# Attention head start regrouped: four tiles in one group, masks by matmul there, and a new order of the whole queue

## The chip, the cores and the metric

The kernel runs on one core of a Trainium2 chip. The metric is device time in microseconds (us), median of several runs.

## What is computed

Two stages follow each other. The first is attention with a local window of 96 keys and 8 global keys, causal, with a distance bias per head; the second is an FFN whose hidden layer is the maximum of three projections.

```python
B, H, S, D = 4, 8, 768, 64
scores = scale * q @ k.T                       # per batch and head
is_global = pos[None, :] < 8
is_local = (rel >= 0) & (rel < 96)             # rel = query - key
keep = is_global | is_local
dist = where(is_global & ~is_local, 96, abs(rel))
scores = scores - slopes[h] * dist             # slopes 2**-(h+1)
scores = where(keep, scores, -1e9)
a = softmax(scores)
x = (a @ v).reshape(3072, 512)                 # tokens x (heads x 64)
h = max(x @ w1, x @ w2, x @ w3)                # 512 -> 768
out = h @ w_out                                # 768 -> 512
```

## The kernel before

The 3072 tokens are 24 tiles of 128, six to a batch. Because of the window, a tile of queries needs only its own keys and those of the tile before (tile t = 0 of a batch: its own alone); the 8 global keys are copied over the first 8 keys of the previous tile, which the window never reaches.

One queue, the string SCHEDULE (L25), sets the order of everything. Each word is a unit: a letter and numbers, the last of which often picks the engine (0 ACT, 1 DVE, 2 POOL). Every engine takes its instructions in this order; SP issues nearly all DMAs in it. The units:

- l: load a part of q or k for a group of neighbouring tiles (`load_part`, L151). Tokens are dealt to partitions so that each partition reads `sz` neighbouring tokens in one run of `sz` x 256 bytes. c casts it to bf16 (`cast_part`, L178), x transposes it on TensorE and evicts it into qkT (`u_x`, L226). Groups (L91) are [first tile, tiles]: [0,2], [2,2], [4,2], [6,4], [10,2].
- L, C, X: the same for single tiles 12 to 23 (L160, L185, L245); X with 4 is a DMA transpose issued by SP. v and C with middle number 1: load and cast v.
- K: wmask, the factor exp(-slope x distance) for a head, on ACT (L297). B: the same bias as an addend for the scores (`u_B`, L291). G, V: copy global keys and values.
- S: scores of a tile for four heads (one g of two) into a PSUM tile sp, then one exp on ACT to P (`u_S`, L268). With its last number 1 the bias is first put into sp by a matmul (L275), and M then does nothing; otherwise M multiplies P by wmask on DVE (`u_M`, L302). In the old queue six of the score units of tiles 0 to 3 have the 1.
- A: P times v and a column of ones, then division on DVE to xb (`u_A`, L311). T: transposes xb to xT (`u_XT`, L335), on TensorE or, with 4, by DMA.
- w, W: load and cast w1 to w3. w g.j loads projection j: g = 0 the first 256 hidden columns, g = 1 the other 512, which two W units cast. o, Q: w_out.
- F c.f.j: projection j of the 128 hidden columns f for the tiles of chunk c: 4 matmuls into one of three PSUM buffers h; j = 0 is evicted by ACT, j = 1 and 2 by a maximum on DVE (`u_F1`, L355). O: second layer of one tile and its store (`u_F2`, L385). E: the last four tiles (L390).
- D: n matmuls on zeros (L432).

Chunks (L89) are 4, 2, 2, 4, 4, 4, 4 tiles: F units work on 512 or 256 columns.

[...] two tiles of two banks for scores and attention output (tags sp0, sp1), three buffers of one bank (tag h, used by F, O and early transposes) and one (tag tp).

Of the kernel before, what the change touches and what calls it, by code (L numbers as in the profile page):

```python
# [12 lines left out]
FP32 = mybir.dt.float32  # L13
# [12 lines left out]
    K0 K1 K2 K3 K4 K5 l1.0 l1.1 D0.3 c0.0.2 B0.1 B1.1 B2.1 B3.0 K6 B4.1 B5.1 c0.1.1 c1.0.2 x0.0.4 B6.1  # L26
    B7.1 x0.1.4 S0.0.1 v0 l2.0 l2.1 K7 S0.1.1 G0.0 S1.0.1 S1.1.0 x1.0.3 c1.1.2 M0.0 M0.1 M1.0 v1 x1.1.4
    C0.1.2 v2 A0.1 G1.2 S2.0.1 M1.1 c2.0.2 x2.0.1 C1.1.1 S2.1.0 G2.2 S3.0.1 M2.0 M2.1 C2.1.1 T0.1 S3.1.1
    M3.0 M3.1 c2.1.2 v3 A1.0 C3.1.0 w0.0 V1.2 x2.1.2 w1.0 A2.1 V2.2 A3.0 T1.0 T2.1 T3.1 W1.0.1 W0.0.0
    G3.2 S4.0.0 S4.1.0 F0.0.0 F0.1.0 M4.0 F0.2.0 F0.3.0 G4.1 S5.0.0 M4.1 S5.1.0 w0.1 W0.1.1 w0.2 W0.2.2  # L30
    V3.2 F0.0.1 F0.1.1 F0.0.2 F0.1.2 v4 C4.1.0 A4.0 V4.2 w1.1 W1.1.2 W2.0.0 F0.4.0 F0.5.0 M5.0 M5.1 w1.2
    W1.2.2 v5 W2.1.0 T4.0 F0.2.1 F0.3.1 l3.0 l3.2 F0.4.1 l3.1 c3.0.2 c3.2.2 F0.5.1 o2 C5.1.0 A5.1 l3.3
    F0.2.2 Q2.2 F0.3.2 W2.2.0 o0 T5.0 F0.4.2 o1 F0.5.2 x3.0.0 F1.0.0 F1.1.0 c3.1.1 F1.2.0 x3.2.0 Q0.2
    F1.0.1 F1.1.1 F1.2.1 l4.0 l4.1 c3.3.0 F1.0.2 F1.1.2 F1.2.2 x3.1.2 x3.3.1 F1.3.0 F1.4.0 Q1.2 F1.3.1
    S6.0.0 S6.1.0 v6 v7 v8 G6.0 F1.3.2 F1.5.0 v9 c4.0.1 F1.4.1 S7.0.0 S7.1.0 G7.2 v10 M6.0 M6.1 M7.0
    M7.1 O0.0.0 F1.4.2 c4.1.1 C6.1.2 C7.1.2 L12 F1.5.1 S8.0.0 S8.1.0 x4.0.0 O0.1.0 A6.0 x4.1.2 A7.1 V7.2
    F1.5.2 v11 T6.0 O0.2.0 T7.1 G8.2 C8.1.2 S9.0.0 S9.1.0 G9.1 v12 v13 O0.3.0 F2.0.0 F2.1.0 S10.0.0 M8.0
    M8.1 M9.0 M9.1 S10.1.0 C9.1.2 L13 L14 F2.0.1 F2.1.1 F2.0.2 A8.0 C12.0.1 F2.1.2 G10.2 O1.0.0 V8.2
    A9.1 X12.1 M10.0 M10.1 C10.1.0 C11.1.0 F2.2.0 S11.0.0 S11.1.0 M11.0 M11.1 L15 F2.3.0 F2.4.0 O1.1.0
    V9.2 A10.1 F2.2.1 V10.2 T8.0 F2.3.1 F2.5.0 T9.0 A11.1 F2.4.1 T10.0 F2.2.2 F2.3.2 T11.1 F2.4.2  # L40
    S12.0.0 S12.1.0 F2.5.1 C13.0.2 C14.0.2 C15.0.1 X13.4 F3.0.0 F3.1.0 F3.0.1 G12.1 C12.1.0 F3.2.0
    F3.1.1 F3.2.1 S13.0.0 S13.1.0 F2.5.2 v14 C13.1.0 C14.1.2 M12.0 M12.1 F3.0.2 F3.1.2 X14.4 F3.2.2
    X15.4 G13.2 M13.0 M13.1 S14.0.0 S14.1.0 F3.3.0 F3.4.0 F3.5.0 M14.0 M14.1 G14.1 A12.0 A13.1 F3.3.1
    F3.4.1 F3.5.1 S15.0.0 M15.0 S15.1.0 G15.0 v15 V13.2 L16 L17 v16 T12.4 v17 M15.1 O2.0.0 C15.1.0 A14.0
    V14.2 F3.3.2 F3.4.2 T13.4 F3.5.2 C16.1.0 C16.0.2 X16.3 T14.4 C17.0.2 A15.1 X17.4 O2.1.0 S16.0.0
    S16.1.0 G16.1 L18 V15.2 L19 T15.1 M16.0 O3.0.0 M16.1 F4.0.0 F4.1.0 F4.0.1 F4.1.1 C18.0.2 L20 C19.0.2
    A16.1 F4.2.0 F4.3.0 S17.0.0 S17.1.0 F4.2.1 F4.0.2 F4.3.1 v18 M17.0 v19 M17.1 X18.3 X19.4 C20.0.0
    V16.2 F4.1.2 C17.1.2 O3.1.1 A17.1 F4.2.2 F4.3.2 S18.0.0 M18.0 S18.1.0 M18.1 F4.4.0 T16.4 T17.4
    F4.4.1 C18.1.2 C19.1.1 F4.4.2 X20.4 G18.1 S19.0.0 S19.1.0 F4.5.0 L21 M19.0 M19.1 v20 F4.5.1 A18.0
    T18.4 F4.5.2 A19.1 T19.4 V19.1 C21.0.1 X21.4 G19.1 L22 C22.0.2 L23 X22.4 O3.2.1 O3.3.0 O4.0.1  # L50
    S20.0.0 S20.1.0 M20.0 G20.0 O4.1.0 F5.0.0 F5.1.0 F5.2.0 S21.0.0 S21.1.0 G21.2 F5.0.1 F5.1.1 M20.1
    M21.0 F5.3.0 F5.0.2 F5.1.2 F5.2.1 F5.2.2 v21 C20.1.1 C21.1.2 F5.4.0 S22.0.0 M21.1 S22.1.0 C23.0.0
    F5.3.1 M22.0 M22.1 F5.5.0 F5.3.2 A20.0 V20.2 G22.2 v22 F5.4.1 X23.4 v23 F5.5.1 T20.4 A21.1 V21.1
    T21.4 F5.4.2 F5.5.2 S23.0.0 S23.1.0 M23.0 O4.2.0 M23.1 C22.1.2 A22.0 C23.1.0 O4.3.0 V22.2 T22.4
    A23.1 T23.4 O5.0.1 O5.1.0 O5.2.1 O5.3.0 F6.0.0 F6.1.0 F6.0.1 F6.0.2 F6.2.0 F6.3.0 F6.4.0 F6.1.1
    F6.2.1 F6.1.2 F6.3.1 F6.4.1 F6.2.2 F6.3.2 F6.5.0 F6.4.2 F6.5.1 F6.5.2 E
# [4 lines left out]
def kernel(  # L61
# [27 lines left out]
    sizes = [4, 2, 2, 4, 4, 4, 4]  # L89

    GROUPS = [[0, 2], [2, 2], [4, 2], [6, 4], [10, 2]]  # L91
# [8 lines left out]
    NSTART = sizes[0]  # L100
# [21 lines left out]
    zeros = persist.tile([128, 512], BF16, name="zeros")  # L122
# [3 lines left out]
    bias = persist.tile([128, 2, 2, 2, 3, 128], BF16, name="bias")  # L126
    NVA = 4
    va_ring = [persist.tile([128, H * 65], BF16, name=f"va{i}") for i in range(NVA)]
    va_first = [persist.tile([128, H * 65], BF16, name=f"vaf{i}") for i in range(2)]
    kg8 = [persist.tile([128, NP, NG], BF16, name=f"kg8_{i}") for i in range(2)]  # L130
# [4 lines left out]
    xT = {}  # L135
    va, masked = {}, {}
# [7 lines left out]
    def part(n, s):  # L144

        T0, sz = GROUPS[n]
        jn = {2: 4, 4: 2, 6: 1}[sz]
        a, x = divmod(s, 4 // jn)
        return divmod(T0, NT) + (sz, a, x * jn, jn)

    def load_part(n, s):  # L151

        bb, t0, sz, a, j0, jn = part(n, s)
        r = raw_pool.tile([128, 2 * DM], FP32, name="rawp", tag="raw")
        r = r[:, 0:sz * jn * 128].rearrange("i (h x) -> i h x", h=2 * jn)
        raw["p", n, s] = r
        src = (q, k)[a][bb, 2 * j0:2 * (j0 + jn), t0 * 128:(t0 + sz) * 128, :]
        nc.sync.dma_start(out=r, in_=src.rearrange("h (i e) d -> i h (e d)", e=sz))
# [19 lines left out]
    def cast_part(n, s, how):  # L178
        bb, t0, sz, a, j0, jn = part(n, s)
        qk = cast_pool.tile([128, 2 * DM], BF16, name="qkp", tag="qkb")  # L180
        qk = qk[:, 0:sz * jn * 128].rearrange("i (e h d) -> i e h d", e=sz, d=D)
        qb["p", n, s] = qk
        copies[how](qk, raw["p", n, s].rearrange("i h (e d) -> i e h d", e=sz))  # L183
# [42 lines left out]
    def u_x(n, s, how):  # L226
# [14 lines left out]
        for (lo, hi, pool, tag, copy), tp in zip(halves, tps):  # L241

            copy(dst[:, lo:hi], tp.rearrange("c e j i -> c j i e"))  # L243
# [24 lines left out]
    def u_S(T, g, how):  # L268
# [3 lines left out]
        if how:  # L272

            for hh in range(2):
                nc.tensor.matmul(sp[:, hh, :, 0:n], identb,  # L275
                                 bias[:, g, hh, :, 0:2] if t else bias[:, g, hh, :, 2:3],
                                 start=True, stop=False, skip_group_check=True)
        for ds in range(2 if t else 1):
            for j2 in range(2):
                jp = 2 * g + j2  # L280
                for hh in range(2):
                    hsl = slice(64 * hh, 64 * hh + 64)
                    nc.tensor.matmul(sp[:, hh, j2, ds], qT(T - ds, 1)[hsl, jp], qT(T, 0)[hsl, jp],  # L283
                                     start=not how, stop=True, skip_group_check=True)
        P = p_pool.tile([128, 4, 2, 128], BF16, name="P", tag="P")
        Pt[T, g] = P
        masked[T, g] = how
# [3 lines left out]
    def u_B(h, how):  # L291
        g, hp = divmod(h, 4)
        j2, hh = divmod(hp, 2)
        mul = (nc.scalar.mul, nc.vector.tensor_scalar_mul, nc.gpsimd.tensor_scalar_mul)[how]
        mul(bias[:, g, hh, j2], rbase, -slopes[h] / scale)

    def u_K(h):  # L297
        g, hp = divmod(h, 4)
        j2, hh = divmod(hp, 2)
        nc.scalar.activation(wmask[:, g, 2 * hh + j2], rbase, AF.Exp, bias=0.0, scale=-slopes[h])  # L300

    def u_M(T, g):  # L302
        P = Pt[T, g]
        if masked[T, g]:
            return
        if T % NT:
            nc.vector.tensor_mul(P, P, wmask[:, g, :, 0:2])  # L307
        else:
            nc.vector.tensor_mul(P[:, :, 0], P[:, :, 0], wmask[:, g, :, 2])

    def u_A(T, how):  # L311

        b, t = divmod(T, NT)
        op = psS.tile([128, 2, 512], FP32, name="op", tag=f"sp{how}")
        for g in range(2):
            P = Pt[T, g]
            for j2 in range(2):
                for hh in range(2):
                    h = 4 * g + 2 * j2 + hh
                    i = 2 * hh + j2  # L320
                    o = op[:, g, (2 * j2 + hh) * 65:(2 * j2 + hh) * 65 + 65]
                    nc.tensor.matmul(o, P[:, i, 0], heads(va[T])[:, h], start=True, stop=(t == 0),  # L322
                                     skip_group_check=True)
                    if t:
                        nc.tensor.matmul(o, P[:, i, 1], heads(va[T - 1])[:, h], start=False, stop=True,  # L325
# [4 lines left out]
        o4 = op[:, :, 0:260].rearrange("p g (h e) -> p g h e", e=65)  # L330
        nc.vector.reciprocal(rz, o4[:, :, :, 64])
        nc.vector.tensor_tensor(out=x.rearrange("p (g h) d -> p g h d", g=2), in0=o4[:, :, :, 0:64],  # L332
                                in1=rz[:, :, :, None].to_broadcast([128, 2, 4, D]), op=ALU.mult)

    def u_XT(T, how):  # L335
        c, i = where[T]
        if i == 0:
            xT[c] = xT_pool.tile([128, NP, len(chunks[c]) * 128], BF16, name="xT", tag="xT")
        if how == 4:
            nc.sync.dma_start_transpose(out=xT[c][:, :, i * 128:(i + 1) * 128],  # L340
                                        in_=xb[T].rearrange("p h d -> p (h d)"))
# [8 lines left out]
        copies[how](xT[c][:, :, i * 128:(i + 1) * 128], tp)  # L350
# [4 lines left out]
    def u_F1(c, f, j):  # L355
        W = len(chunks[c]) * 128
        if f == 0 and j == 0:
            ht[c] = ht_pool.tile([128, NF, W], BF16, name="ht", tag="ht")
        ps = psH.tile([128, W], FP32, name="h", tag="h")
        for dm in range(4):  # L360
            nc.tensor.matmul(ps, w123[f // 2][:, dm, j, (f % 2) * 128:(f % 2) * 128 + 128],  # L361
                             xT[c][:, dm], start=(dm == 0), stop=(dm == 3))
        if j == 0:
            h01 = h01_pool.tile([128, W], BF16, name="h01", tag="h01")
            h01s[c, f] = h01
            nc.scalar.copy(h01, ps)  # L366
        elif j == 1:
            nc.vector.tensor_max(h01s[c, f], h01s[c, f], ps)  # L368
# [141 lines left out]
```

The softmax here doesn't subtract the row's maximum and nothing guards it: scores larger than these inputs give would overflow.

## Time and profile before

| what | us |
|---|---|
| median of 3 runs | 180.45 (180.34 to 180.5) |
| span of the profiled execution | 178.5 |
| outside the span (median less span) | 1.95 |
| first FFN matmul (h, L361) | 23.27 |
| L361: 491 matmuls recorded, chain share | 53% |
| L376: second layer, chain share | 16% |
| DVE: 36 mask products L307, mean | 0.716 |
| ACT: 40 exps of 128x1024 L288, mean | 1.027 |

The span runs from the first to the last instruction of the core. Busy time of TensorE includes the modelled end of each matmul; starts in the chain of waits are the better measure of what one matmul costs in a stream. Single long rows of the timeline, such as "x8", merge several instructions.

### The profile page before, as it was taken

The numbers are of one execution on the slowest core, as the hardware profiler recorded it, in microseconds if no ns is written. First come the engines' busy times: TensorE is split into PE (matmuls) and PEld (weight loads), VectorE is DVE, ScalarE is ACT, GpSimd is POOL, SyncE is SP. The second block draws the span as 40 slices with busy tenths as digits, with TensorE's granted clock in tenths as the row PEclk, the third lists the DMA queues.
The fourth block names the chain that finished last, engine by engine and source line by source line (L and its number), as shares of the span: only waits on it lengthen the run. The fifth ranks groups of instructions, "written<-read, shape, count | busy, mean of one in ns | idle before, by whom it ended". The sixth has DMA issues, their size and how long they took to land.

```text
span 178.5 us, 3963 instructions
## 1 busy us (share of the span) xinstructions
PE 167.1 (94%) x1529; PEld 95.9 (54%) x1551; DVE 119.1 (67%) x237; ACT 103.2 (58%) x160; POOL 37.4 (21%) x65
## 2 busy tenths in 40 slices
PE   3599799999999999999999999999999999999991
PEld 0455645458866677845555555454454555444451
DVE  4519975977796689748978448978358986137610
ACT  4867898646689958555753936351862543440131
POOL 4255203543343012210006024100020401000000
PEclk9999999999999999999999999999999999999998
DMA  5999999999998899899544999988989664700015
GB/s 139 292 270 243 357 321 383 319 361 356 252 194 229 218 254 227 142 204 234 92 90 122 167 253 231 145 172 152 182 156 300 123 129 147 252 12 4 0 47 190
DMA packets 83587, 35.52 MB, mean 199 GB/s; under 512 B 66160, under 2 KB 78320, under 8 KB 83568
## 3 DMA queue, kind: packets, MB, share of 16 engines
q1 hardware_dynamic: 83424, 35.20, 83.6%
q8 instruction: 12, 0.20, 0.5%
q10 hardware_dynamic: 144, 0.07, 0.1%
q14 instruction: 7, 0.06, 0.1%
HBM read 25.17 MB, written 6.29 MB: 176 GB/s over the span
## 4 chain that ended last, share of the span: by engine, by line
PE 88%; ACT 3%; DVE 2%; POOL 2%; issue 1%; DMA 1%; POOLq 0%; ACTq 0%
PE h L361 53%; PE po L376 16%; PE sp L283 7%; PE op L322 3%; PE op L325 3%; PE tpp L239 3%; PE xtp L349 2%; ACT wmask L300 2%; PE sp L275 2%; DMA out_dram<-ost 1%; DVE qkT L243 1%; DVE xb L332 1%; ACT ost L382 1%; ACT P L288 1%; PE tp L261 1%
## 5 line engine op out<-in xcount | busy, mean ns | idle before, releaser
L361 PE MATMUL h<-xT,w 128*128 128x512 bf16 (+1 forms) x491 | 99.2, 348 | 0.7 <-issue 0.2
L361 PEld LDWEIGHTS <-w 128*128 128x128 bf16 x504 | 47.0, 98 | 40.4 <-ACT w L427 0.2
L288 ACT ACTIVATE P<-sp 128x1024 bf16<-128x1024 f32 (+1 forms) x48 | 43.4, 954 | 20.4 <-PE sp L283 20.2
L368 DVE TENSOR_TENSOR h<-h,h 128x512 bf16<-128x512 bf16 (+1 forms) x42 | 25.2, 609 | 25.6 <-PE h L361 15.5
L366 ACT CAST h<-h 128x512 bf16<-128x512 f32 (+1 forms) x42 | 21.6, 532 | 21.5 <-PE h L361 21.3
L376 PE MATMUL po<-wo,ht 128*128 128x512 bf16 (+2 forms) x147 | 33.1, 362 | 0.5
L370 DVE TENSOR_TENSOR ht<-h,h 128x512 bf16<-128x512 bf16 (+1 forms) x42 | 25.0, 606 | 3.7 <-PE h L361 3.0
L307 DVE TENSOR_TENSOR P<-P,wmask 128x1024 bf16<-128x1024 bf16 x36 | 24.8, 716 | 3.6 <-ACT P L288 3.5
L382 ACT COPY ost<-po 128x512 f32<-128x512 f32 (+2 forms) x20 | 11.2, 564 | 18.4 <-PE po L376 11.2
L376 PEld LDWEIGHTS <-ht 128*128 128x128 bf16 x156 | 14.0, 98 | 13.8
L332 DVE TENSOR_TENSOR xb<-op,rz 128x512 bf16<-128x512 f32 x24 | 16.6, 691 | 0.8
L283 PEld LDWEIGHTS <-qkT 64*128 64x128 bf16 x352 | 10.2, 96 | 10.0 <-issue 8.0
L283 PE MATMUL sp<-qkT 64*128 64x128 bf16 x352 | 15.2, 223 | 0.4 <-DVE xb L332 0.4
L322 PEld LDWEIGHTS <-P 128*128 128x128 bf16 x192 | 12.5, 97 | 2.7 <-ACT P L288 0.2
L221 POOL COPY va<-vaf 8x260 int32<-8x260 int32 x14 | 6.3, 449 | 34.7 <-PE op L325 34.7
L198 POOL CAST qkb<-raw 128x1024 bf16<-128x1024 f32 x7 | 7.2, 1037 | 27.6 <-DMA raw<-in_k_dram 27.6
L322 PE MATMUL op<-va,P 128*128 128x65 bf16 x160 | 12.4, 193 | 0.3 <-ACT va L189 0.2
L239 PE MATMUL tpp<-identb,qkp 128*128 128x128 bf16 x96 | 8.5, 246 | 4.0 <-POOL qkp L183 3.5
L325 PEld LDWEIGHTS <-P 128*128 128x128 bf16 x160 | 10.4, 97 | 1.8 <-issue 0.2
L239 PEld LDWEIGHTS <-qkp 128*128 128x128 bf16 x96 | 7.0, 112 | 5.8 <-POOL qkp L183 4.4
L325 PE MATMUL op<-va,P 128*128 128x65 bf16 x128 | 9.9, 193 | 0.1
L243 ACT COPY qkT<-tpp 128x1024 bf16<-128x1024 bf16 (+1 forms) x9 | 7.9, 873 | 3.4 <-PE tpp L239 3.4
(66 smaller groups left out, 107.7 us busy)
## 6 DMA issues: line engine op xcount, KB each, us to landing
rawv<-in_v_dram SPq DMA_DIRECT2D x24, 256.0 KB, 4.9
out_dram<-ost SPq DMA_DIRECT2D x23, 256.0 KB, 2.3
rawp<-in_q_dram SPq DMA_DIRECT2D x6, 512.0 KB, 7.3
rawp<-in_k_dram SPq DMA_DIRECT2D x6, 512.0 KB, 7.7
wst<-in_moe_w_dram SPq DMA_DIRECT2D x3, 1024.0 KB, 10.3
raw<-in_q_dram SPq DMA_DIRECT2D x12, 256.0 KB, 4.2
raw<-in_k_dram SPq DMA_DIRECT2D x12, 256.0 KB, 4.7
wst<-in_moe_w_dram SPq DMA_DIRECT2D x3, 512.0 KB, 8.6
```

Source lines behind the costliest of these rows:

```text
L239: nc.tensor.transpose(tp[:, e, j - lo], qb["p", n, s][:, e, 2 * j:2 * j + 2].rearrange("i h d -> i (h d)"), identb)
L283: nc.tensor.matmul(sp[:, hh, j2, ds], qT(T - ds, 1)[hsl, jp], qT(T, 0)[hsl, jp], start=not how, stop=True, skip_group_check=True)
L288: nc.scalar.activation(P[:, :, 0:n], sp.rearrange("p a b d n -> p (a b) d n")[:, :, 0:n], AF.Exp, bias=0.0, scale=scale)
L307: nc.vector.tensor_mul(P, P, wmask[:, g, :, 0:2])
L322: nc.tensor.matmul(o, P[:, i, 0], heads(va[T])[:, h], start=True, stop=(t == 0), skip_group_check=True)
L325: nc.tensor.matmul(o, P[:, i, 1], heads(va[T - 1])[:, h], start=False, stop=True, skip_group_check=True)
L332: nc.vector.tensor_tensor(out=x.rearrange("p (g h) d -> p g h d", g=2), in0=o4[:, :, :, 0:64], in1=rz[:, :, :, None].to_broadcast([128, 2, ...
L361: nc.tensor.matmul(ps, w123[f // 2][:, dm, j, (f % 2) * 128:(f % 2) * 128 + 128], xT[c][:, dm], start=(dm == 0), stop=(dm == 3))
L366: nc.scalar.copy(h01, ps)
L368: nc.vector.tensor_max(h01s[c, f], h01s[c, f], ps)
L370: nc.vector.tensor_max(ht[c][:, f], h01s[c, f], ps)
L376: nc.tensor.matmul(po, ht[c][:, f, tt * 128:(tt + 1) * 128], wo[:, f, cols], start=(f == 0), stop=(f == NF - 1))
```

## The change

Three things change together.

*The first four tiles.* They become one group (GROUPS [0,4]), loaded in 8 parts (q and k, four head pairs each) of four neighbouring tokens per partition, 1 KB runs. Queries stay in the order in which the tokens were dealt (token 4i+e in place e x 32 + i of its tile), so for q the eviction is contiguous; keys are put in natural order as before. Stores of these tiles are written back to the right rows.

*Their scores.* `u_S` with bias is gone. A new unit s works on a head pair for two tiles: the bias goes in by a matmul whose stationary operand is the identity scaled by the head's slope (diag) and whose moving operand is the distance table (rbaseb); then the score matmuls, then one exp. There is no M for tiles 0 to 3. Tile 3's view of tile 2's keys with the global keys in front is a separate tile k2x; the small unit g makes these copies.

*Sizes and order.* Chunks become 2, 2, 2, 2, 4, 4, 4, 4, so F works on 256 columns for the first eight tiles; two neighbouring small chunks share one xT and one ht. A with last number 2 takes two h buffers in place of a score tile. The dummy matmuls are 128 columns wide, 46 of them. K units move behind, B units go, and the whole queue has a new order. Of the tiles 12 to 23, 11 instead of 9 have their q and k transposed by DMA.

```diff
 SCHEDULE = """
-    K0 K1 K2 K3 K4 K5 l1.0 l1.1 D0.3 c0.0.2 B0.1 B1.1 B2.1 B3.0 K6 B4.1 B5.1 c0.1.1 c1.0.2 x0.0.4 B6.1
-    B7.1 x0.1.4 S0.0.1 v0 l2.0 l2.1 K7 S0.1.1 G0.0 S1.0.1 S1.1.0 x1.0.3 c1.1.2 M0.0 M0.1 M1.0 v1 x1.1.4
-    C0.1.2 v2 A0.1 G1.2 S2.0.1 M1.1 c2.0.2 x2.0.1 C1.1.1 S2.1.0 G2.2 S3.0.1 M2.0 M2.1 C2.1.1 T0.1 S3.1.1
-    M3.0 M3.1 c2.1.2 v3 A1.0 C3.1.0 w0.0 V1.2 x2.1.2 w1.0 A2.1 V2.2 A3.0 T1.0 T2.1 T3.1 W1.0.1 W0.0.0
-    G3.2 S4.0.0 S4.1.0 F0.0.0 F0.1.0 M4.0 F0.2.0 F0.3.0 G4.1 S5.0.0 M4.1 S5.1.0 w0.1 W0.1.1 w0.2 W0.2.2
...
+    l0.5 c0.5.1 l0.0 D5.28 K5 D3.9 x0.5.3 l0.4 c0.4.1 K7 K1 g2.1.2 c0.0.0 K6 x0.0.2 x0.4.0 D2.9 g2.0.0
+    s0.0.0 g1.0.1 l0.2 c0.2.2 l0.7 l0.1 c0.7.1 c0.1.1 K3 l0.6 c0.6.2 s1.0.1 v1 l0.3 x0.1.1 s0.1.0 x0.2.1
+    g1.1.2 c0.3.2 x0.6.3 s0.2.1 x0.3.3 C1.1.2 g1.2.1 x0.7.2 s0.3.1 g2.3.0 v0 s1.1.0 C0.1.2 A0.2 w0.1.0
+    v2 K0 g1.3.2 s1.3.1 G0.2 A1.2 v3 g2.2.2 s1.2.0 T0.0 C2.1.2 G3.2 C3.1.1 w0.0.0 W0.0.0 K4 T1.1 V1.2
+    W0.1.1 A2.1 V2.2 A3.0 T2.0 F0.0.0 T3.1 V3.2 F0.0.1 w1.0.0 W1.0.2 W2.0.0 F0.1.0 F1.0.0 F1.1.0 F1.4.0
+    F1.1.1 w0.2.0 l1.0 c1.0.2 F1.2.0 F0.4.0 W0.2.1 F1.0.1 F1.1.2 F0.1.1 F0.0.2 F1.3.0 x1.0.4 F1.0.2 l1.1
...
+    T21.4 V21.0 C22.1.2 F6.3.1 A22.1 V22.1 F6.3.2 F6.5.2 S23.1 M23.1 S23.0 O5.1.1 M23.0 O6.0.0 T22.4
+    O6.3.0 A23.0 T23.4 O6.1.0 O5.3.1 O6.2.1 F7.0.0 F7.1.0 F7.1.1 F7.2.0 F7.0.1 F7.1.2 F7.4.0 F7.4.1
...
-    sizes = [4, 2, 2, 4, 4, 4, 4]
-
-    GROUPS = [[0, 2], [2, 2], [4, 2], [6, 4], [10, 2]]
+    sizes = [2, 2, 2, 2, 4, 4, 4, 4]
+
+    GROUPS = [[0, 4], [4, 2], [6, 4], [10, 2]]
...
+    BIG = [0, 0, 1, 1, 2, 3, 4, 5]
...
-        jn = {2: 4, 4: 2, 6: 1}[sz]
+        jn = 1 if n == 0 else {2: 4, 4: 2, 6: 1}[sz]
...
+    def u_g(T, jp, how):
+
+        k0 = qT(0, 1)[:, jp, 0:NG]
+        if T == 1:
+            copies[how](qT(1, 1)[:, jp, 0:NG], k0)
+        else:
+            copies[how](k2x[:, jp, NG:128], qT(2, 1)[:, jp, NG:128])
+            copies[how](k2x[:, jp, 0:NG], k0)
+
+    def u_s(tp, jp, how):
+
+        sp = psS.tile([128, 2, 4, 128], FP32, name="sp", tag=f"sp{how}")
...
+        lo = 0 if tp else 1
+        bb = rbaseb[:, None, 1:3].to_broadcast([128, 2, 2, 128]) if tp else rbaseb
+        for hh in range(2):
+            nc.tensor.matmul(sp[:, hh, lo:4], diag[:, 2 * jp + hh], bb, start=True, stop=False, skip_group_check=True)
+        for i, T in enumerate(tiles):
+            for ds in range(2 if T else 1):
+                for hh in range(2):
...
+                    nc.tensor.matmul(sp[:, hh, 2 * i + ds if T else 1], ks, qs,
+                                     start=False, stop=True, skip_group_check=True)
...
+        nc.scalar.activation(P[:, :, lo:4], sp[:, :, lo:4], AF.Exp, bias=0.0, scale=scale)
...
+        if how == 2:
+            ops = [psH.tile([128, 512], FP32, name="op", tag="h") for _ in range(2)]
...
+            if W < 512:
+                h01s[c, f] = h01_pool.tile([128, W], BF16, name="h01s", tag="h01s", bufs=8)
...
-            nc.tensor.matmul(wp, zeros[:, 0:128], zeros, start=True, stop=True)
+            nc.tensor.matmul(wp[:, 0:128], zeros, zeros, start=True, stop=True)
...
-        load_part(0, 0)
-        load_part(0, {2: 1, 4: 2, 6: 4}[GROUPS[0][1]])
...
+        for h in range(4):
+            nc.vector.tensor_scalar_mul(diag[:, h], identf, -slopes[h] / scale)
...
+        for h in range(4, H):
+            nc.vector.tensor_scalar_mul(diag[:, h], identf, -slopes[h] / scale)
...
+        nc.vector.tensor_copy(rbaseb, rbase)
```

## The prediction

> **What bounds the kernel now.** I read the busy lines of the page first, then the chain of waits, then the engines' busy time in four stretches, then the timeline of the first 24 us. Columns of a windows line: the stretch, its length, busy us (instructions) of PE, PEld, DVE, ACT, POOL, then granted clock, DMA share, GB/s.
>
> ```profile
> span 178.5 us, 3963 instructions
> PE 167.1 (94%) x1529; PEld 95.9 (54%) x1551; DVE 119.1 (67%) x237; ACT 103.2 (58%) x160; POOL 37.4 (21%) x65
> ...
> PE 88%; ACT 3%; DVE 2%; POOL 2%; issue 1%; DMA 1%; POOLq 0%; ACTq 0%
> ```
>
> ```profile
> 0.00:7.69 7.69, 2.49 (x12) 1.13 (x12) 3.63 (x20) 5.37 (x11) 3.23 (x13) 1.00 0.81 203
> 7.69:23.27 15.58, 14.25 (x197) 9.32 (x198) 11.01 (x22) 11.75 (x17) 6.03 (x10) 1.00 1.20 294
> 23.27:174.85 151.58, 150.31 (x1324) 85.46 (x1344) 104.23 (x196) 85.80 (x132) 28.14 (x42) 1.00 0.82 190
> 174.85:178.50 3.65, 0.00 (x0) 0.00 (x0) 0.24 (x1) 0.27 (x1) 0.00 (x0) 0.84 0.43 147
> ```
>
> TensorE is the bound from 23.27 us (the first FFN matmul) to 174.85, and nearly without gaps. Before 23.27 it isn't: it waits, or runs slowly. The chain shows on what (start, us, what), first early, then later for comparison:
>
> ```profile
> 3.76 2.59 ACT wmask L300 x6
> ...
> 7.69 1.01 PE tpp L239 x8
> ...
> 12.25 0.98 PE tpp L239 x8
> ...
> 23.70 3.18 PE h L361 x14
> ...
> 33.42 3.45 PE h L361 x16
> ...
> 41.04 0.45 PE tpp L239 x8
> ...
> 43.24 2.62 PE h L361 x24
> ```
>
> Eight transposes take 0.98 us at 12.25 and 0.45 us at 41: the early ones run at half speed. The timeline has the marks of the first stretch:
>
> ```profile
> 0.74 0.45 SPq L158 DMA_DIRECT2D rawp<-in_q_dram  x1
> ...
> 5.09 1.04 POOL L183 CAST qkp<-rawp 128x1024 bf16<-128x1024 f32 x1 [2.01 <-DMA rawp<-in_q_dram]
> ...
> 9.50 0.60 ACT L288 ACTIVATE P<-sp 128x512 bf16<-128x512 f32 x1 [0.60 <-PE sp L283]
> ...
> 23.27 2.97 PE L361 MATMUL h<-xT,w 128*128 128x512 bf16 x12
> ```
>
> So: what TensorE must do, priced at full speed, and how much earlier its steady part can begin.
>
> **Work on TensorE.** Prices from the chain: a 512-wide h matmul 3.45/16 = 0.216 us, a 256-wide one 2.62/24 = 0.109, a transpose 0.45/8 = 0.056, a score matmul 0.55/16 = 0.034, an op matmul 0.03. Before 23.27 the old queue does 48 qk transposes (2.7), 72 score matmuls (2.5), 8 bias matmuls of 512 and 4 of 256 columns (2.2), 56 op matmuls (1.7), 16 xb transposes (0.9): 10.0 us. So 13.2 us of the head are lost. The rest, priced likewise, is 149.2; it takes 151.6: 2.4 us lost in 150. The prize is the head.
>
> [...] 290 GB/s at 5 to 9 us, when q and k come in 512-byte runs, 226 at 16 to 18 us with v in 256-byte runs, 389 at 21 to 22 us with weights in runs of 1 to 2 KB. [...] an h buffer is reused only after its eviction. Here that eviction is 0.42 us on DVE for 256 columns and 0.69 for 512, against 0.44 and 0.86 us of matmuls.
>
> **The change part by part.**
>
> *TensorE's total.* One chunk of 512 becomes two of 256: 36 x 0.437 for 18 x 0.8625, +0.2. Mask matmuls: from 2.2 to eight of 384 columns (0.162) and eight of 512: 3.0, +0.8. Transposes of later tiles: X units on TensorE fall from 3 to 1, 16 x 0.056 = -0.9. Dummies of the start lie in time that is lost anyway. Net about +0.2; no gain here.
>
> *Loads.* Data flow begins about 3.2 us (5.05 landing, less 0.52 MB at 290). A part of the new group is 256 KB in 1 KB runs; I take 375 GB/s, near the weights' rate, bounds 290 and 389. The first part lands at 3.9 instead of 5.05. Ahead of the first weights for use stand 2.1 MB of q and k (5.6), 1.05 MB of v at 226 (4.6) and two w0 loads (2.8): the second w0 lands at 16.2, w1.0 at 19.0, the third w0 at 20.4. Tiles 4 and 5, loaded in the old queue before v1, now come after these.
>
> *Constants.* In the old queue six wmask exps (2.59), then a bias scaling and another exp, stand on ACT before the first eviction. Now three K units (1.3) stand before the first cast; the rest are spread out. Eight bias scalings (2.4) leave; eight diag scalings of 128x128 come (not shown; between the 0.15 of a 128x128 copy and the 0.35 of the 128x384 scaling; I take 0.2, so 1.6), partly in DVE's 0.87 us wait for POOL, plus one 128x384 copy (0.3). DVE is free about 4.0, against 3.65.
>
> *First exp.* Cast 0.42 to 4.4; the dummies, 37 at 0.107 cold from 1.19, hold TensorE to 5.1 [...]; transposes; interleaved eviction on DVE 0.68 to 6.0; second cast to 6.4; its transposes to 6.7; ACT eviction 0.58 to 7.3; two key copies 0.4; scores: first exp at 7.85, against 9.50.
>
> *From there ACT sets the pace.* Before its first FFN eviction it must do four exps of 768 columns (0.75, between the rows of 512 and 1024), four of 1024 (0.97 back to back, from a pair of 1.94), two wmask (0.9), one eviction of 512 (0.6), two key copies (0.4), one xT copy (0.6) and the w cast (1.05): 10.5 us. I find about 0.9 of waiting, for transposed k of the third and fourth pair, which DVE evicts. FFN can begin at 7.85 + 10.5 + 0.9 = 19.2; w0 landed at 16.2, so DMA isn't last. By then TensorE has done 32 + 12 transposes (2.5), 56 score (1.9), mask (3.0) and 56 op matmuls (1.7): 9.1. Head lost: 10.1 instead of 13.2, a gain of 3.1. The fourth tile's transpose waits for its division on DVE: give back 0.3.
>
> *After that.* Over the next 30 us of TensorE work the new queue puts on DVE 33 units of 256 (13.7), 6 mask products of 1024 and 2 of 512 (5.2), 4 divisions (4.2), 5 casts and evictions (3.4) and 3 xT copies (1.3): 27.8 us; the old one 23.9 (trace: 22.8, as neighbours overlap). ACT: 26.0 against 25.3. So DVE goes from 76% to 88%, in strict order, with three h buffers. I put the new waits at 0.6 us; bounds -1.5 (most of the old 2.4 gone) and +2. Casts of w1 lag their need by 1.4 us or more: w1.0 at 19.0, its ACT cast not before 20.4. The late part (two more DMA transposes of qk, 2 x 1.25 us of SP) shifts nothing I can see: SP has idle stretches there. At the end the transpose of tile 23 is covered by three F2 units (3.9 us) instead of four (5.2); it needs 0.9 for the division and 2.4 to land, up to 3.7. Cost 0, up to 0.7.
>
> *Sum.* TensorE ends at 19.2 + 0.3 + 150.2 + 2.4 + 0.6 = 172.7 instead of 174.85; the tail of 3.65 is untouched: span 176.35. The median is 1.95 above the span of the profiled execution; with that, **178.3**.
>
> **Rivals.** *DVE and ACT take over (slower).* While FFN units are 256 wide, a long operation (0.6 to 1.2 us) ahead of an eviction can exceed the 0.87 us that the other two h buffers give. The stretch of 256-wide units is 48 us of TensorE work, with 28 such operations on DVE and 38 on ACT. At 0.08 us each they cost 5.3 us: 178.3 - 0.6 + 5.3 = 183.0; it decides from 2.75/66 = 0.04 us each. For it: DVE at 88%, and more evictions per us. Against: the old 256-wide stretch has 57 of them in 39 us, the same density, and TensorE was busy 26.74 of 27.0 us from 49 to 76. *Loads late.* If 1 KB runs come at 290 as the old ones, w0 lands at 18.6, w1.0 at 22.2 and the third w0 at 24.0; the casts then wait 0.6 and 1.8, together about 1.9 us of TensorE: 180.2. Against: the weights' 389. *The order closes the old gaps too:* 1.5 us of the 2.4 go, and no new waits: 176.2. That the change does nothing is no rival: what stands before the first exp is different on every engine.
>
> **How the numbers follow.** Forecast 0.57 (its own range 176.9 to 179.8), slower rival 0.20, late loads 0.10, closed gaps 0.13. A measurement of this kernel tells about 0.2%, 0.36 us, from no change. Faster: 0.57 + 0.13 + nearly half of the late loads = 0.74; same 0.06; slower 0.20. The range holds all but the worse half of the slower rival and the edge of the best case: 175.8 to 182.4.
>
> **What would show it.** First exp near 7.9 us; ACT hardly idle from there to 19; first h matmul at 19.2 +- 0.8, with TensorE warm from about 5; then busy lines as dense as before, PE ending near 172.7. Wrong, if first h comes after 21.5, or if PE waits for h buffers (evictions on DVE) add over 3 us between 20 and 65 us, or if a wait for wst stands before h.

## The result and the profile after

| kernel | us, median | ratio to before, 95% interval |
|---|---|---|
| before | 180.47 (180.34 to 180.52) | 1 |
| after | 193.37 (192.07 to 194.7) | 1.0716 [1.0664, 1.0769] |

The change makes the kernel 12.9 us slower, where 2.2 us less were forecast. Two single runs of the experiments below were slow and are left out: one with four stores per tile (202.3 us, at a granted clock of 0.847; it is the profiled one, so that profile isn't read) and one with tiles 18 and 19 on TensorE (191.25 us).

The page of the changed kernel, first its busy lines, then slices of TensorE's busy time, clock and DMA share, then the shares of the chain:

```profile
span 190.3 us, 4220 instructions
PE 172.1 (90%) x1654; PEld 104.7 (55%) x1654; DVE 123.3 (65%) x269; ACT 103.8 (55%) x166; POOL 38.9 (20%) x68
...
PE   7669799899999999999997059999999999999992
...
PEclk9999999999999999999999759999999999999999
DMA  5999999999889899986969899599999511720006
...
PE 75%; DVE 9%; ACT 7%; DMA 5%; issue 2%; POOL 0%; ACTq 0%; POOLq 0%; DVEq 0%
```

TensorE has a hole in slices 22 and 23, at 104 to 114 us, and its clock falls there. DMA has 5% of the chain where it had 1%. The stretches (columns as in the prediction) put a size to it:

```profile
4.91:21.53 16.62, 12.32 (x184) 7.61 (x183) 8.90 (x24) 15.02 (x24) 6.41 (x17) 1.00 1.12 314
21.53:103.50 81.97, 80.51 (x887) 56.33 (x884) 63.84 (x138) 53.27 (x88) 24.74 (x32) 1.00 0.96 225
103.50:111.40 7.90, 0.40 (x8) 0.23 (x8) 0.82 (x2) 1.09 (x2) 0.00 (x0) 0.75 0.96 105
111.40:186.64 75.24, 74.82 (x544) 36.61 (x544) 45.84 (x83) 31.73 (x49) 5.31 (x8) 0.98 0.63 136
```

In 7.9 us TensorE works 0.4 us, and no other engine is busy for more than 1.1. TensorE's waits (what waited, for what: us in total, times, longest), and the chain there:

```profile
PE h L418 <- DMA xT<-xb: 7.0, 1, 7.0
...
PE sp L293 <- DMA qkT<-qkb: 0.9, 1, 0.9
```

```profile
103.20 0.35 DVE ost L444
103.56 7.84 DMA xT<-xb
111.39 0.05 issue
111.44 3.30 PE h L418 x8
```

One DMA transpose, of tile 15, takes 7.84 us from issue to landing, and the first F unit of the chunk with tiles 12 to 15 waits for it. The eight 512-wide matmuls after it take 3.30 us, 0.41 each in place of 0.216: TensorE has gone cold (its granted clock is 1.00 up to 106 us, 0.87 from there to 108, and 0.50 from 108 to 114), which costs another 1.6 us. SP's timeline shows what stood ahead of that transpose:

```profile
93.24 0.59 SPq L446 DMA_DIRECT2D out_dram<-ost  x1
93.93 1.35 SPq L397 DMA_TRANSPOSE xT<-xb  x1
95.38 1.81 SPq L446 DMA_DIRECT2D out_dram<-ost  x1
97.28 5.54 SPq L266 DMA_TRANSPOSE qkT<-qkb  x2
102.92 0.54 SPq L446 DMA_DIRECT2D out_dram<-ost  x1
103.56 1.26 SPq L397 DMA_TRANSPOSE xT<-xb  x1
```

Between the transposes stand the stores of tiles 0, 1 and 2, three of the four that are written in the new row order (each is 256 KB). Issuing two qk transposes takes SP 5.54 us (L266), and the transposes from 87 to 106 us land after 6.4 us (xT, median of three) and 6.7 (qkT, of three). The one that is issued ahead of these three stores, at 91.87, lands after 3.4. In the kernel before, seven xT transposes from 85 to 130 us took (first line), against those of the changed kernel:

```profile
DMA to landing us min/median/max: 2.4/2.4/3.7
```

```profile
DMA to landing us min/median/max: 3.4/6.4/7.8
```

What the DMA engines do while only such stores and transposes are under way is seen in three half-microseconds, picked out of the stretch from 98.5 to 101 us:

```profile
99.50:100.00 0.50, 0.50 (x4) 0.21 (x3) 0.18 (x1) 0.24 (x1) 0.00 (x0) 1.00 0.26 85
100.00:100.50 0.50, 0.50 (x4) 0.26 (x3) 0.50 (x1) 0.00 (x0) 0.00 (x0) 1.00 0.31 83
100.50:101.00 0.50, 0.50 (x4) 0.21 (x3) 0.40 (x2) 0.00 (x0) 0.00 (x0) 1.00 0.29 105
```

The last two columns are DMA share and GB/s: a share of 0.26 to 0.31, at 83 to 105 GB/s. The share is no count of engines: the two other half-microseconds of that stretch have 0.27 and 0.46, and from 101.5 to 102 us it is 2.41. What sets the new store apart is its destination, `rows.rearrange("(i e) c -> e i c", e=4)`, whose slowest dimension is 4. Whether that makes it slow, this profile alone doesn't show; the experiments vary it.

**The head** gained nothing. The first exp starts at 9.06 us and the first h matmul at 21.53, in a steady stream only from 22.85. With the prices of the prediction, 13.1 us are lost by then (before: 13.2; forecast: 10.4).

```profile
4.00 2.38 ACT L344 ACTIVATE wmask<-rbase 128x384 bf16<-128x384 f32 x3 [1.77 <-DVE rbase L539]
...
9.06 0.81 ACT L333 ACTIVATE P<-sp 128x768 bf16<-128x768 f32 x1
```

Three K units take 2.38 us here, not 1.3.

### The profile page after: what moved, and what is told of

The parts are those of the page before. It is cut to its first block, busy times and chain, and to the rows that moved or that the text cites. A ratio compares the mean times of both kernels' runs of the same rounds, so it can differ in the third digit from the quotient of the medians.

```text
span 190.3 us, 4220 instructions
## 1 busy us (share of the span) xinstructions
PE 172.1 (90%) x1654; PEld 104.7 (55%) x1654; DVE 123.3 (65%) x269; ACT 103.8 (55%) x166; POOL 38.9 (20%) x68
## 4 chain that ended last, share of the span: by engine, by line
PE 75%; DVE 9%; ACT 7%; DMA 5%; issue 2%; POOL 0%; ACTq 0%; POOLq 0%; DVEq 0%
PE h L418 45%; PE po L438 15%; PE sp L293 5%; DMA xT<-xb 4%; PE op L367 3%; DVE P L350 2%; PE tpp L251 2%; ACT P L333 2%; PE op L370 2%; ACT wmask L344 2%; PE xtp L405 1%; DMA out_dram<-ost 1%; DVE ht L431 1%; DVE h01s L429 1%; DVE xb L386 1%
## 5 line engine op out<-in xcount | busy, mean ns | idle before, releaser
L418 PE MATMUL h<-xT,w 128*128 128x256 bf16 (+1 forms) x576 | 103.8, 329 | 8.1 <-DMA xT<-xb 7.0
L429 DVE TENSOR_TENSOR h<-h,h 128x512 bf16<-128x512 bf16 x24 | 16.4, 684 | 24.5 <-PE h L418 11.9
L427 ACT CAST h<-h 128x512 bf16<-128x512 f32 x24 | 14.1, 587 | 30.2 <-PE h L418 30.0
L431 DVE TENSOR_TENSOR ht<-h,h 128x512 bf16<-128x512 bf16 x24 | 16.3, 681 | 3.2 <-PE h L418 2.5
L386 DVE TENSOR_TENSOR xb<-op,rz 128x512 bf16<-128x512 f32 x19 | 13.1, 691 | 0.7
L367 PE MATMUL op<-va,P 128*128 128x65 bf16 x160 | 12.6, 193 | 0.2
L429 DVE TENSOR_TENSOR h01s<-h01s,h 128x256 bf16<-128x256 bf16 x24 | 9.7, 415 | 4.5 <-PE h L418 2.5
L201 POOL CAST va<-rawv 128x512 bf16<-128x512 f32 x12 | 7.8, 652 | 20.9 <-DMA rawv<-in_v_dram 8.6
L427 ACT CAST h01s<-h 128x256 bf16<-128x256 f32 x24 | 8.8, 378 | 4.7 <-PE h L418 4.2
L370 PEld LDWEIGHTS <-P 128*128 128x128 bf16 x160 | 10.5, 97 | 1.2
L431 DVE TENSOR_TENSOR ht<-h01s,h 128x256 bf16<-128x256 bf16 x24 | 9.7, 416 | 2.1 <-PE h L418 1.5
L195 POOL CAST qkp<-rawp 128x1024 bf16<-128x1024 f32 (+1 forms) x10 | 9.7, 972 | 6.0 <-DMA rawp<-in_q_dram 3.0
```

The costliest lines, as they stand in the source:

```text
L367: nc.tensor.matmul(o, get_P(T, g, j2, hh, 0), heads(va[T])[:, h], start=True, stop=(t == 0), skip_group_check=True)
L370: nc.tensor.matmul(o, get_P(T, g, j2, hh, 1), heads(va[T - 1])[:, h], start=False, stop=True, skip_group_check=True)
L386: nc.vector.tensor_tensor(out=x4, in0=o4[:, :, :, 0:64], in1=rz[:, :, :, None].to_broadcast([128, 2, 4, D]), op=ALU.mult)
L429: nc.vector.tensor_max(h01, h01, ps)
L431: nc.vector.tensor_max(ht[B][:, f, o], h01, ps)
```

## The experiments

Theories held against each other: *stores* (the pattern of the first four tiles' stores slows the DMAs behind them), *crowding* (too many transposes on SP at 92 to 105 us, stores or not), *mask reads* (the K units read the distance table in dealt order, one element every 128 bytes, and lengthen the head), *DVE pace* (DVE with 256-wide evictions sets the pace after the head).

**Plain stores.** The rows of the first four tiles are left in the order in which the partitions hold them. Edit to the changed kernel:

```diff
-        dma.dma_start(out=rows.rearrange("(i e) c -> e i c", e=4) if T < 4 else rows, in_=ost)
+        dma.dma_start(out=rows, in_=ost)
```

> The stores of the first four tiles write their rows in the order in which the partitions hold them, so the rows of these four tiles come out in another order within their 512 tokens; all else is as after the change. Theory S (the stores with rows four apart are slow and hold up the transposes that follow them in the same DMA queues): the 7 us wait of the h matmuls for xT goes, the transposes between 93 and 112 us land in 2.4 to 4.5 us again as in the kernel before, time near 184. Theory Q (too many DMA transposes follow each other there): no change beyond 1 us, 193.

Measured: 183.03 us, 1.0146 [1.0129, 1.0163]. Among TensorE's waits none is for a DMA any more; the largest, all but the last in the head:

```profile
PE tpp L251 <- ACT qkp L195: 1.4, 1, 1.4
...
PE op L370 <- POOL va L233: 0.8, 2, 0.5
PE h L418 <- DVE w L494: 0.6, 1, 0.6
```

and the same two qk transposes are issued in 2.67 us, tile 15's 4.6 us earlier:

```profile
95.54 2.67 SPq L266 DMA_TRANSPOSE qkT<-qkb  x2
98.31 0.53 SPq L446 DMA_DIRECT2D out_dram<-ost  x1
98.93 1.22 SPq L397 DMA_TRANSPOSE xT<-xb  x1
```

The store's pattern alone is 10.3 of the 12.9 us (1.0716 less 1.0146, times 180.4), 2.6 us for each of four stores on average. With as many transposes in the same places, crowding is refuted as the main cause.

**Fewer transposes on SP.** Tile 15's transpose goes to TensorE, later in the queue; in another kernel those of q and k of tiles 18 and 19 do (parts of lines of the queue):

```diff
-    A15.0 T15.4 F4.0.2 F4.5.0 X16.4 T14.0 C17.1.1
+    A15.0 F4.0.2 F4.5.0 X16.4 T14.0 T15.0 C17.1.1
```

> One unit, the transpose of tile 15's xb, is made by TensorE instead of DMA, placed three FFN units later. Both theories S and Q expect the wait of 7.0 us before the first FFN unit of tiles 12 to 15, and the half clock after it, to go: 193.4 - 7.0 - 1.6 + 0.2 = 185. If the time stays over 190, the wait has only moved to another late transpose (X18 for the scores of tile 18).

```diff
-    A14.0 V14.1 X18.4 X19.4 F4.3.2
+    A14.0 V14.1 X18.3 X19.3 F4.3.2
```

> The q and k transposes of tiles 18 and 19 are made by TensorE instead of DMA (16 transposes, +0.9 us of TensorE work, as one of the two was in the kernel before). Theory Q: with only T12, T13, T15 and X16 left there, the transposes land in under 4.5 us, and the 7 us wait goes: about 193.4 - 7 - 1.6 + 0.9 = 186. Theory S: T13 and T15 stay slow (over 6 us) behind the stores of tiles 0 to 2, and at least 3 us of the wait remain: 189 to 193.

Measured: 190.88 us, 1.0572 [1.0545, 1.0598], and 188.94 us (median of three runs), 1.0472 [1.0435, 1.0508]. The 185 us expected of the first didn't come. Neither removes the wait; it moves (first kernel) or shrinks (second):

```profile
PE sp L293 <- DMA qkT<-qkb: 4.4, 1, 4.4
```

```profile
PE h L418 <- DMA xT<-xb: 3.4, 1, 3.4
```

So taking out the transpose that TensorE waits for shows the next late one.

**Which feature of the store.** Two causes are held apart: S1, the form with 4 blocks of 32 rows, and S2, rows that lie 8 KB apart. Both kernels write the first four tiles differently; in the first the row step stays 8 KB in DRAM but the slowest dimension is 128 (rows come out in another order), in the second four stores of 32 rows each go to the right rows:

```diff
+        if T < 4:
+            rows = out[0:512, cols].rearrange("(i t) c -> t i c", t=4)[T]
```

> The stores of tiles 0 to 3 write single rows four apart (8 KB from row to row) in one two-dimensional pattern of 128 rows; the rows of these tiles come out in another order within their 512 tokens. Theory S1 [...]: here the store has 128 rows in its outer dimension [...], time as with plain stores, near 183. Theory S2 (rows 8 KB apart are slow to write): as slow as after the change, 191 to 194.

```diff
+            for e in range(4):
+                dma.dma_start(out=rows.rearrange("(i e) c -> e i c", e=4)[e], in_=ost[32 * e:32 * e + 32])
```

> The stores of tiles 0 to 3 become four stores each, of 32 partitions and 64 KB, to the right rows; what is computed is the reference. S1: [...] time 183 to 184.5, with three more SP issues of 0.36 us per tile. S2: no change, 191 to 194.

Measured: 183.08 us, 1.0149 [1.0125, 1.0174], and 1.0236 [1.0205, 1.0268] (184.0 to 185.1 us). Scattered rows cost nothing against the plain store; four DMAs in place of one give back 8.7 us of the 10.3. What is slow here is neither the addresses nor the rows, but one DMA whose slowest dimension is 4.

**The size of that dimension.** The same three-dimensional form with 16 blocks of 8 rows and with 8 blocks of 16 (`e=16` and `e=8` in place of `e=4`). In both, the first forecast takes the count of blocks as the cause:

> The changed kernel, with the stores of tiles 0 to 3 in a pattern of 16 blocks of 8 rows in place of 4 blocks of 32; rows of these tiles come out in another order. [...] 183.0 us as with the plain store, 182.5 to 183.6, and no wait of TensorE for a DMA over 1 us. If any three-dimensional destination is slow, the time stays at 191 to 195.

> The same with 8 blocks of 16 rows. [...] a store alone runs at about twice the rate of 4 blocks (170 to 210 GB/s, share near 0.5), half the extra time is gone and the kernel lies well below the middle, 183.5 to 187.5, since the transposes then wait less than the cover they have. Any three-dimensional destination: 191 to 195.

| blocks | us | ratio | xT transposes, 85 to 112 us: landing, median | longest wait of TensorE for a DMA |
|---|---|---|---|---|
| 4 | 193.37 | 1.0716 [1.0664, 1.0769] | 6.4 | 7.0 |
| 8 | 187.36 | 1.0383 [1.0366, 1.0401] | 4.2 | 3.3 |
| 16 | 182.52 | 1.012 [1.0107, 1.0134] | 2.8 | none |
| plain, 128 rows | 183.03 | 1.0146 [1.0129, 1.0163] | 2.5 | none |

Three dimensions as such cost nothing (16 blocks: 182.52 us, plain: 183.03); the count does, in order. With 8 blocks 45% of the extra time against 16 blocks is left (4.8 of 10.9 us): near half, though not well below the middle, as was expected. The share near 0.5, the author's estimate, shows in some half-microseconds (0.45 and 0.55 from 99 to 100 us), the doubled rate does not (32 and 111 GB/s there). With 8 blocks the chain still shows the transpose of tile 15:

```profile
100.78 6.31 DMA xT<-xb
107.09 0.04 issue
107.13 2.84 PE h L418 x8
```

**The pattern in the kernel before.** Stores of tiles 6 to 9 of the old kernel in the pattern of 4 blocks (rows of these tiles in another order):

```diff
+        dma.dma_start(out=rows.rearrange("(i e) c -> e i c", e=4) if 6 <= T < 10 else rows, in_=ost)
```

> The kernel before, with the stores of tiles 6 to 9 (issued between 93 and 113 us, near DMA transposes) in the pattern of 4 blocks of 32 rows; their rows come out in another order within each tile. S (such a store alone is slow and holds what follows it in the DMA queues): slower than 180.35 by 1 to 8 us, with transposes between 93 and 120 us landing in over 5 us instead of 2.4 to 4.4. If the pattern is harmless by itself: 180.1 to 180.7.

Measured: 187.78 us, 1.0419 [1.0367, 1.047]. Nothing else of the change is in this kernel, and its TensorE is hit where the transposes follow, again with a fallen clock:

```profile
PE h L361 <- DMA xT<-xb: 2.4, 1, 2.4
```

```profile
100.00:110.00 10.00, 7.58 (x42) 3.15 (x40) 3.43 (x6) 2.83 (x5) 0.46 (x1) 0.83 0.95 165
```

The kernel before in the same stretch:

```profile
100.00:110.00 10.00, 9.84 (x80) 5.11 (x80) 5.33 (x10) 5.78 (x9) 2.98 (x4) 1.00 1.12 243
```

The pattern costs 7.4 us there: it is the store, not the new order, that does the harm. The six xT transposes from 85 to 130 us land after 4.0 us (median), the seven of the kernel before after 2.4. They aren't the only DMAs that it holds up. SP takes 4.07 us to issue a load at 103.01 that took it 1.31 in the kernel before, and its queue falls behind: a load of k is issued at 127.26 (before: 117.96), DVE waits 2.99 us for it, and TensorE 1.8 us for a copy that stands behind it on DVE.

**The mask reads.** POOL first copies the distance table into natural order, and K reads that copy:

```diff
+        nc.gpsimd.tensor_copy(rnat.rearrange("p s (i e) -> p s i e", e=4),
+                              rbase.rearrange("p s (e i) -> p s i e", e=4))
```

> The wmask exps read a copy of the distance table in natural order, made once by POOL, instead of the dealt order. Theory W (the strided read makes each of the seven exps before the first FFN matmul take 0.79 to 0.88 us instead of 0.43 to 0.51, and ACT sets the pace of the head): each goes back to 0.5, the first h matmul comes 2 to 2.8 us earlier, near 20.5, and the time falls by about 2.5 to 191. If ACT doesn't set the pace there: first h within 0.7 us of 22.85, no change of time.

Measured: 193.38 us, 1.0722 [1.0674, 1.077], no gain. The groups of the K exps (form, busy us, mean ns | idle before), first with the dealt order (the line is of the plain-store kernel, whose K units are those of the changed kernel), then of this one:

```profile
L344 ACT ACTIVATE wmask<-rbase 128x384 bf16<-128x384 f32 x8 | 6.8, 874 | 1.8 <-DVE rbase L539 1.8
```

```profile
L345 ACT ACTIVATE wmask<-rnat 128x384 bf16<-128x384 f32 x8 | 4.0, 518 | 2.8 <-POOL rnat L541 2.8
```

The exps are as cheap as expected, but they start 1.0 us later, behind POOL's copy, and the first cast on DVE, which runs beside that copy, takes 1.07 us:

```profile
4.21 1.07 DVE L196 CAST qkp<-rawp 128x512 bf16<-128x512 f32 x1
```

It takes 0.42 without it. And TensorE was cold at 7 us here (eight transposes in 1.03 us) and not in the profile of after (0.62, see the end), so this run does not settle what the reads cost.

**Queries in natural order.** The interleaving of queries is undone at their eviction; distance tables, mask reads and stores are then all contiguous, the rest of the change stays:

```diff
-            if n == 0 and a == 0:
-                copy(batch_T(0)[:, 0, j0 + lo:j0 + hi, 0:sz * 128].rearrange("c j (e i) -> c j e i", e=sz),
-                     tp.rearrange("c e j i -> c j e i"))
...
-                       pattern=[[1, 4], [4, 32]], channel_multiplier=-1,
+                       pattern=[[1, 128]], channel_multiplier=-1,
...
-        dma.dma_start(out=rows.rearrange("(i e) c -> e i c", e=4) if T < 4 else rows, in_=ost)
+        dma.dma_start(out=rows, in_=ost)
```

> Queries of the first four tiles are put in natural order at their eviction, as keys are; so the stores are plain, the distance tables are in natural order and the wmask exps read them contiguously; three DVE evictions cost 0.68 instead of 0.42 us. Store theory S: at most 183.5. Theory W (strided wmask exps set the pace of the head): 1 to 2.5 us less than with plain stores alone, 180.5 to 182, with the first h matmul near 20 instead of 21.5. If the head is held by something else, first h after 21 and time 182.5 to 184.

Measured: 181.11 us, 1.0068 [1.0043, 1.0093]. ACT in the head:

```profile
3.94 1.35 ACT L340 ACTIVATE wmask<-rbase 128x384 bf16<-128x384 f32 x3 [1.71 <-DVE rbase L534]
...
8.08 0.81 ACT L329 ACTIVATE P<-sp 128x768 bf16<-128x768 f32 x1
...
10.54 0.81 ACT L329 ACTIVATE P<-sp 128x768 bf16<-128x768 f32 x1 [0.33 <-PE sp L320]
12.60 0.81 ACT L329 ACTIVATE P<-sp 128x768 bf16<-128x768 f32 x1 [1.25 <-PE sp L320]
```

K units cost 0.45 each, the first exp comes at 8.08 (forecast 7.85), and the stream at 21.75, 1.1 us before that of the changed kernel. Two of the waits between exps are in brackets: ACT waits 1.25 us for scores that need transposed q or k from DVE. This is the best version of the change, and it is still 0.7 us behind the kernel before. Its thirteen runs fall in two groups, eight from 180.9 to 181.6 us and five from 182.2 to 183.0; the profile is of the first group, and why there is a second isn't known. In that profile the head loses 12.0 us (1.2 less than before), but up to A23.0 (150.32 us) another 4.1 go, where the kernel before loses 2.4 up to its end.

**Closing single waits of that version.** Eleven units of the last kernel's queue moved, in the first kernel near 20 and 30 us, in the second near 139 us too, such as (parts of lines)

```diff
-    A3.0 T2.0 F0.0.0 T3.1 V3.2 F0.0.1 w1.0.0 W1.0.2 W2.0.0 F0.1.0 F1.0.0
+    A3.0 T2.0 F0.0.0 F0.1.0 F0.0.1 T3.1 V3.2 w1.0.0 W1.0.2 W2.0.0 F1.0.0
...
-    G4.2 W2.1.1 F0.1.2 F1.5.1 M4.1
+    G4.2 F0.1.2 W2.1.1 F0.5.0 F1.5.1 M4.1
...
-    G21.2 S22.0 M22.0 S22.1 G22.1 C23.0.2 M22.1 F6.5.0 X23.4 F6.5.1 F6.3.0
+    G21.2 S22.0 F6.5.0 S22.1 G22.1 C23.0.2 F6.5.1 M22.0 M22.1 X23.4 F6.3.0
```

> The kernel with natural queries and plain stores (181.1 us), with eleven units of its queue moved near 20 and 30 us: three F units before the transpose of tile 3, where TensorE waits for a division; F0.1.2 before the cast W2.1.1, and F0.5.0 and F0.5.1 as cover before F1.5.1 and A4.1, whose waits were 0.4 and 0.7 us. If what that kernel still lacks against the old one are single waits in the 20 to 36 us stretch, about 1.3 us go: 179.8, and the loss when A4.1 starts falls from 13.3 us to about 12. If DVE as a whole sets the pace there, the waits come back a few units later and the time stays at 180.9 to 181.3.

> As the run before, and in addition F6.5.0 and F6.5.1 stand before the last two mask products of tile 22, near 139 us, where TensorE waited 0.7 us for the eviction behind them. Single waits: another 0.6 us less, 179.2. DVE as the pace: no less than the run before it. If F6.5.1's earlier place only delays A22 and the attention behind it, 0.3 us more than the run before it.

Measured: 183.09 us, 1.0159 [1.0141, 1.0176], and 182.85 us, 1.0136 [1.0114, 1.0157]; the intervals overlap, so the late move shows neither gain nor loss. The early ones cost 2 us against the median of the kernel that they start from, half a us against its slower group. A4.1 starts at 37.42 us with 22.7 us of priced work done: 14.7 lost in place of 13.3. Its waits for weight casts (TensorE, first kernel):

```profile
PE h L413 <- DVE w L489: 1.3, 2, 0.7
...
PE h L413 <- ACT w L489: 0.7, 1, 0.7
```

TensorE's wait for M4.0 has given way to these, since the evictions moved forward stand ahead of the casts on ACT and DVE. That fits DVE and ACT as the pace better than single waits. But 0.5 us of it was there before the first moved unit (the third exp at 11.04, behind a part of q that landed later), so how much is the order and how much the head isn't separated. No version here beats the kernel before.

## Why the prediction was wrong

- **The step that failed:** "The late part (two more DMA transposes of qk, 2 x 1.25 us of SP) shifts nothing I can see: SP has idle stretches there." It counted the time in which SP issues, and took the landing of the transposes as unchanged. The stores of tiles 0 to 3, whose destination the change makes three-dimensional, were given no cost at all. In its place the runs show 10.3 us: a store of 256 KB with a DMA share of 0.26 to 0.31 beside it in three half-microseconds, xT transposes behind it that land after 6.4 and 7.8 us instead of 2.4 to 3.7, the second of them on the path for 7.0 us, and a cold TensorE after that (granted clock 0.50, 1.6 us).
- **A second term, too small:** "three K units (1.3)". They took 2.38. They read in the dealt order, each element 128 bytes from the last; the eight exps take 0.874 us each so and 0.518 from a table in natural order. First exp 9.06 against 7.85; with natural reads 8.08.
- **ACT's pace:** from first exp to first h, 10.5 us of work and 0.9 of waits were forecast; measured were 12.47 us, of which ACT was busy 10.92. The waits are 1.55, 0.65 more. ACT is not alone in setting the pace: DVE's evictions of transposed q and k hold it in part (TensorE waits 0.6 us for one of them, and ACT 0.98 for the scores after it).
- **Tile 3's division:** 0.3 us forecast. From the first h to the stream are 1.32 us with four matmuls (0.44) in them: 0.9 lost.
- **What held:** TensorE warm at 6.9 us in the profile of after (eight transposes in 0.62 us; with the same dummies ahead it was cold in the plain-store kernel, 1.03 us); the first load (the first cast at 4.21 against a forecast landing of 3.9 and DVE free at 4.0); the tail as before (3.66 us).
- **What held by luck:** no wait of TensorE in the list is for a load, but loads were late. The second w0 was issued at 11.46 and landed 7.1 us later, at 18.6: not the 16.2 of the forecast, but the figure of the rival "loads late". DMA moved 322 GB/s from 5 to 9 us and 278 from 9 to 14, not 375. It cost nothing that the waits show, because ACT came to the cast of that w0 at 20.12 only.
- **The slower rival**, evictions on DVE and ACT at 256 columns, gave 183.0. Without the slow stores the kernel does take 183.0, but mostly not for that reason. Of the plain-store kernel's losses 13.8 us lie in the head (forecast 10.4) and 4.3 between the stream and A23.0; the forecast had 3.0 for the whole rest, the rival 7.7. By this profile some 1.3 us speak for its mechanism, and 3.4 for a head that gains nothing. The split isn't firm: its TensorE was cold in the head (1.03 us for eight transposes at 6.96). The kernel with rows 8 KB apart has the same queue; its stream starts at 22.45 instead of 23.59, yet its A23.0 at 152.53 instead of 152.29. It loses 12.7 in the head and 5.7 after it. So an earlier stream was not carried to the end, which fits a pace set by other engines; but the sign that the rival named, over 3 us of waits for h buffers, didn't come (one wait of 0.7 in the list of the changed kernel).
- **What would make it wrong:** "if first h comes after 21.5" came true by 0.03 us. The wait that decided was in none of the listed signs, because no rival was about a DMA other than a load.

What stays open: where exactly the last 0.7 us of the natural-query kernel lie. Losses rise slowly (12.0 at the stream, 13.3 at A4.1, 13.9 at A6.2, 15.0 at A15.0, 16.1 at A23.0), at no single wait over 0.7 us.

## What to carry to other kernels

Of every DMA that a change touches, look at the slowest dimension of the destination, not only at bytes and run lengths: here the kernel took 182.5 to 183.1 us where it was 16 or 128, 184.0 to 185.1 with four DMAs of 32 in place of one, 187.4 with 8 and 193.4 with 4; no other count was run. These slow stores had no waiter of their own, so they showed as a late landing of what stood behind them in the same queue (xT 6.4 us in place of 2.5): price moved or changed DMAs by landing time, not by issue time. A layout that makes one copy contiguous can be paid for by those who read in it later; count them (here eight mask exps, 0.874 us each in place of 0.518, a distance table and four stores) before the copy's gain.

## What the runs showed of the hardware

- A store of 4 blocks of 32 rows slowed the transposes issued behind it: median landing of xT 6.4 us with 4 blocks, 4.2 with 8, 2.8 with 16 (2.5 behind plain stores). Why the count of blocks matters, no run shows.
- The same head ran with a warm TensorE in one kernel and a cold one in another, with about the same pause ahead of it (first line after, second the plain-store kernel, whose head is the same):

```profile
6.94 0.62 PE L251 MATMUL tpp<-identb,qkp 128*128 128x128 bf16 x8 [1.55 <-ACT qkp L195]
```

```profile
6.96 1.03 PE L251 MATMUL tpp<-identb,qkp 128*128 128x128 bf16 x8 [1.42 <-ACT qkp L195]
```

  The first exp then came at 9.06 and at 10.08 us. With 16 blocks, and the same head, it came at 9.06 again. The granted clock is 1.00 in the head of the first, and 0.999 over the whole span of the second. What decides between warm and cold isn't shown. Differences of 1 us between heads can be this, and single profiles should not be read finer.
- A DVE cast took 1.07 us beside a POOL copy, 0.42 without. The copy runs from 4.05 to 4.99, the cast from 4.21 to 5.28. Later in that run a cast at 6.59 took 0.42 beside smaller POOL copies (6.74 to 7.28), so whether the first copy is the cause isn't shown.
